# Two expert units multiply three sequence chunks in one float32 pass instead of two, with new engine lists

## The chip, the cores and the metric

The kernel runs on one core of a Trainium2 chip. The metric is the device time of one execution in microseconds (us), the median of several runs. The profile is one more execution, recorded instruction by instruction.

## What is computed

Three stages follow each other: a chunked linear scan (an attention with decay), a gated feed-forward layer, and a second feed-forward layer with a squared ReLU. Cut to what matters:

```python
for c in range(nc):                                   # scan over 768 positions, 4 batches, 8 heads
    M = einsum('bhin,bhjn->bhij', Cc, Bc) * L          # L: decay between positions, causal
    y[:, :, sl] = einsum('bhij,bhjd->bhid', M, xc) + einsum('bhin,bhnd->bhid', Cc, state) * decay_to_i
    state = decay_full * state + sum(Bx)
x = y.transpose(0, 2, 1, 3).reshape(3072, 256)
g = x @ w_gate                                        # 256 x 1536
x = (g * sigmoid(g) * (x @ w_val)) @ w_out            # 1536 x 256
h = maximum(x @ w2_in, 0.0)                           # 256 x 2048
out = (h * h) @ w2_out                                # 2048 x 256
```

The weights arrive as 64-bit words, which the kernel itself turns into float32.

## The kernel before

**The scan.** Each of the four batches is cut into chunks of 112 positions (six, and a last one of 96). A chunk takes, in this order: two transposes of its B and C on TensorE (tile `trb`, L529, from the loaded tile `eb`), the spread of its decays over partitions (`ab`, L616), two scans on VectorE that make `L` (L625), the scores (`cb`, L679), their product with `L` (`mt`, L712), the output product (`ys`, L727), and the transposes of the new state (`turn`, L766), which the next chunk's `ys` needs. So the chunks of a batch follow each other in a chain. The tiles `eb` are two buffers: the load of chunk 2's B and C (L518) goes into the buffer of chunk 0.

**The gated layer of the first batch.** The 1536 hidden columns are six units of gate and value weights (`gv` 0 to 5), each of two blocks of 128. For one block and one piece of positions, TensorE makes the gate product (`g`, L791) and the value product (`v`), ScalarE the SiLU, VectorE the product (L858), and TensorE multiplies it back into the accumulator (`acc`, L905). There are two ways to multiply. Units marked exact use float32 operands as they are (`xf` times `v`, two instructions for the 256 inputs, each of which the trace shows as two records). The others split each operand in a rounded and a rest part (`hi` and `lo`, `xh_all` and `xl_all`) and use three products of parts. Only units 0 and 3 are exact, and only for chunks 0 to 2. The table `cells` says which unit multiplies which chunks: an entry (j, c0, c1, exact) is unit j with chunks c0 to c1 - 1, and the order of the entries is the order of priority. A piece wider than 256 positions takes a PSUM bank each for `g` and `v`, a narrower one takes one for both.

**The other batches** are multiplied in four tiles of 512 positions, and the second layer follows in six tiles of 512; both in split parts.

**Preparing the weights.** Each unit is loaded in two halves (L428) and turned into float32 by ScalarE (L441, L447, and L452 for units so marked) and VectorE (L456, the clamp L462, the shift L466). A string of four digits for each unit in `engs` says: sign on ScalarE, clamp on POOL (GpSimd), rest part on POOL, in halves or whole.

**The order.** A list for each engine (`seq`) names the operations by number, in the order in which the engine issues them. A planner in the kernel gives the buffers. Where the planner has TensorE without work, the program gets dummy products of a tile of zeros (`idle`, L241), a fixed number at each place, written into the tile of the instruction that follows:

```python
for _ in range(fills.pop()):
    nc.tensor.matmul(t, idle[:, : shape[0]], idle[:, : t.shape[-1]], start=True, stop=True)
...
n = (gap - COLD) / 110 + COLD / 216 if free < 1200 else gap / 105
if gap > 150:
    fills.append(int(n) + PLAN["more"] if free < 1200 or op.start > 12000 else int(gap / 216) + 1)
```

They stand in the instruction stream as any other product and run whether TensorE would have waited or not.

Of the kernel before, what the change touches and what calls it, by code (L numbers as in the profile page):

```python
# [141 lines left out]
def kernel(  # L142
# [982 lines left out]
    with tc.manual_schedule():  # L1125
        for op in order:
# [22 lines left out]
        (0, 2, 3, 1),  # L1149
        (3, 1, 3, 1),  # L1150
        (3, 0, 1, 1),
        (2, 0, 3, 0),
        (2, 3, 7, 0),
        (0, 0, 2, 1),
# [9 lines left out]
    engs=['0011', '1001', '1000', '1011', '1011', '1011', '1001', '1000', '0010'],  # L1164
# [7 lines left out]
    rest=[55, 98],  # L1172
# [25 lines left out]
        ],  # L1198
        POOL=[
# [5 lines left out]
        ],  # L1205
        PE=[
# [16 lines left out]
        ],  # L1223
        ACT=[
# [61 lines left out]
```

## Time and profile before

| | |
|---|---|
| median of 3 runs | 627.5 us (627.07 to 627.64) |
| the profiled execution's own time | 627.6 us |
| its span, first to last instruction | 625.9 us |
| TensorE (PE) busy | 619.8 us, 99% of the span |
| VectorE (DVE), ScalarE (ACT), GpSimd (POOL) busy | 424.6, 335.2, 99.4 us |

Busy time is the union of an engine's instructions. The end of a TensorE product is modelled, so its duration is longer than the distance to the next one; what a product costs in a dense stretch is the distance between two starts.

### The profile page before, as it was taken

The page shows a single profiled execution, that of the slowest core. Times are in us where ns is not written, and L with a number is a line of the kernel's source. Part 1 is how long each engine was busy: PE and PEld are TensorE (multiplying, and loading weights), DVE is VectorE, ACT ScalarE, POOL GpSimd, SP SyncE. Part 2 cuts the span into 40 slices and gives each one's busy share as a digit, 9 for nine tenths or more (in the row PEclk, how much of TensorE's full clock was granted, in tenths as well). Part 3 has the DMA queues.
Part 4 walks back from the last instruction along what each step waited for, and adds up shares of the span by engine and source line. Part 5 has one row for each costly group of instructions (what it writes and reads, how often), then busy time and mean ns, then how long its engine had stood idle before and what let it go on. Part 6 is the DMA issues. An engine that isn't in the chain of part 4 may idle for free.

```text
span 625.9 us, 9674 instructions
## 1 busy us (share of the span) xinstructions
PE 619.8 (99%) x3682; PEld 525.1 (84%) x3682; DVE 424.6 (68%) x668; ACT 335.2 (54%) x615; POOL 99.4 (16%) x130
## 2 busy tenths in 40 slices
PE   8999999999999999999999999999999999999997
PEld 6889999998878787878888888888888888888897
DVE  7897888877876866883688985454545554545543
ACT  6898985455443535542476564444444444444443
POOL 2425513313121231211113310000000000000000
PEclk9999999999999999999999999999999999999999
DMA  8879975756656555640224200010010100200101
GB/s 185 212 191 228 209 151 93 132 110 124 135 96 132 99 102 118 148 137 33 68 68 135 68 1 0 1 34 1 9 26 1 35 2 0 35 0 1 34 1 36
DMA packets 153855, 49.85 MB, mean 80 GB/s; under 512 B 141648, under 2 KB 142160, under 8 KB 153808
## 3 DMA queue, kind: packets, MB, share of 16 engines
q1 hardware_dynamic: 153248, 48.87, 35.4%
q8 instruction: 29, 0.48, 0.3%
q10 hardware_dynamic: 560, 0.36, 0.2%
q14 instruction: 18, 0.15, 0.1%
HBM read 34.96 MB, written 3.25 MB: 61 GB/s over the span
## 4 chain that ended last, share of the span: by engine, by line
PE 98%; DMA 1%; DVE 0%; SPq 0%; issue 0%; DVEq 0%
PE h L791 21%; PE g L791 18%; PE acc L977 17%; PE acc L905 16%; PE v L791 14%; PE acc L986 4%; PE ys L727 3%; PE cb L688 2%; PE cb L679 1%; PE ab L616 1%; DMA dv<-in_a_dram 1%; PE trb L529 0%; PE g L241 0%; PE cb L241 0%; PE turn L766 0%; PE ab L241 0%
## 5 line engine op out<-in xcount | busy, mean ns | idle before, releaser
L967 DVE TENSOR_TENSOR p<-t,p 128x512 fp32r<-128x512 f32 x96 | 68.2, 713 | 65.2 <-ACT p L963 65.2
L963 ACT ACTIVATE p<-t 128x512 fp32r<-128x512 f32 x96 | 60.6, 633 | 75.9 <-PE acc L977 53.3
L960 DVE TENSOR_TENSOR t<-t 128x512 f32<-128x512 f32 x96 | 66.2, 691 | 51.6 <-ACT t L957 51.6
L977 PE MATMUL acc<-p,hi 128*128 128x512 f32 x320 | 98.6, 389 | 0.0
L957 ACT ACTIVATE t<-h 128x512 f32<-128x512 f32 x96 | 57.4, 598 | 66.1 <-PE h L791 63.2
L905 PE MATMUL acc<-p,hi 128*128 128x512 f32 (+3 forms) x320 | 90.2, 366 | 0.0
L855 ACT ACTIVATE t<-g 128x512 f32<-128x512 f32 (+5 forms) x88 | 44.8, 516 | 71.9 <-PE g L791 63.9
L791 PE MATMUL h<-xh_all,hi 128*128 128x512 f32 x192 | 74.8, 390 | 0.0
L791 PE MATMUL h<-xl_all,hi 128*128 128x512 f32 x192 | 74.8, 390 | 0.0
L791 PE MATMUL h<-xh_all,lo 128*128 128x512 f32 x192 | 74.7, 389 | 0.0
L878 DVE TENSOR_TENSOR p<-t,p 128x512 fp32r<-128x512 f32 (+3 forms) x80 | 57.4, 727 | 21.0 <-ACT p L873 20.4
L873 ACT ACTIVATE p<-t 128x512 fp32r<-128x512 f32 (+3 forms) x80 | 45.4, 572 | 47.2 <-DVE t L858 38.6
L977 PEld LDWEIGHTS acc<-p,hi 128*128 128x128 f32 x320 | 60.1, 188 | 12.5
L858 DVE TENSOR_TENSOR t<-t,v 128x512 f32<-128x512 f32 (+2 forms) x68 | 43.7, 647 | 36.0 <-PE v L791 26.8
L791 PE MATMUL g<-xh_all,hi 128*128 128x512 f32 (+3 forms) x184 | 65.3, 355 | 0.0
L791 PE MATMUL g<-xl_all,hi 128*128 128x512 f32 (+3 forms) x184 | 64.6, 351 | 0.0
L791 PE MATMUL g<-xh_all,lo 128*128 128x512 f32 (+3 forms) x184 | 64.6, 351 | 0.0
L905 PEld LDWEIGHTS acc<-p,hi 128*128 128x128 f32 x320 | 57.1, 189 | 7.3
L977 PE MATMUL acc<-p,lo 128*128 128x512 f32 x160 | 62.2, 389 | 0.0
L905 PE MATMUL acc<-p,lo 128*128 128x512 f32 (+3 forms) x160 | 57.9, 362 | 0.0
L791 PE MATMUL v<-xh_all,hi 128*128 128x512 f32 (+2 forms) x136 | 51.2, 377 | 0.0
L791 PE MATMUL v<-xl_all,hi 128*128 128x512 f32 (+2 forms) x136 | 51.0, 375 | 0.0
(108 smaller groups left out, 1071.7 us busy)
## 6 DMA issues: line engine op xcount, KB each, us to landing
ab<-decay SPq DMA_DIRECT2D x23, 452.0 KB, 4.2
raw<-in_moe_w_out_dram SPq DMA_DIRECT2D x14, 512.0 KB, 5.5
raw<-in_moe_w_in_dram SPq DMA_DIRECT2D x8, 512.0 KB, 3.8
raw<-in_moe_w_val_dram SPq DMA_DIRECT2D x6, 512.0 KB, 5.2
raw<-in_moe_w_gate_dram SPq DMA_DIRECT2D x6, 512.0 KB, 5.4
xa<-in_x_dram SPq DMA_DIRECT2D x24, 112.0 KB, 3.0
out_dram<-o SPq DMA_DIRECT2D x40, 64.0 KB, 1.9
bc<-in_B_dram SPq DMA_DIRECT2D x18, 56.0 KB, 2.9
```

The source lines that it names most:

```text
L791: nc.tensor.matmul(ps, l, r, start=(i == 0), stop=(i == len(terms) - 1))
L855: nc.scalar.activation(t[:, :n], gg(), AF.Silu)
L858: nc.vector.tensor_tensor(tb.t[:, :n], tb.t[:, :n], vv(), op=ALU.mult)
L873: nc.scalar.activation(p[:, 0, :n], tb.t[:, :n], AF.Copy)
L878: e.tensor_tensor(p[:, 1, :n], tb.t[:, :n], p[:, 0, :n].bitcast(F32), op=ALU.subtract)
L905: nc.tensor.matmul(ps, l, r, start=bank not in done_f, stop=f == NF - 1, skip_group_check=True,)
L957: nc.scalar.activation(new(tb, [P, TN], F32, "t"), ph.t, AF.Relu)
L960: nc.vector.tensor_tensor(tb.t, tb.t, tb.t, op=ALU.mult)
L963: nc.scalar.activation(new(pb, [P, 2, TN], F32R, "p")[:, 0, :], tb.t, AF.Copy)
L967: e.tensor_tensor(pb.t[:, 1, :], tb.t, pb.t[:, 0, :].bitcast(F32), op=ALU.subtract)
L977: nc.tensor.matmul(acc[-1 - i][m], l.t[:, w], pb.t[:, r, :], start=(f == 0 and s == 0), stop=(f == NF2 - 1 and s == 2),)
L986: nc.tensor.matmul(acc[-1 - i][q][:, :256], pb.t[:, l, tk], r, start=(f == 0 and s == 0), stop=(f == NF2 - 1 and s == 2),)
```

## The change

The exact units get one piece of 336 positions (chunks 0 to 2) each, where each had a piece of 112 and one of 224. Unit 0's clamp goes from VectorE to POOL, and the second unit of output weights (`o` 1) is prepared whole and no longer in halves. `rest` changes a bound on the cells that use VectorE for the rest part; with 14 or 12 cells neither 55 nor 99 is reached. All five lists are new.

```diff
     cells=[
         (1, 3, 7, 0),
         (3, 3, 7, 0),
         (4, 3, 7, 0),
-        (0, 2, 3, 1),
-        (3, 1, 3, 1),
-        (3, 0, 1, 1),
+        (3, 0, 3, 1),
         (2, 0, 3, 0),
         (2, 3, 7, 0),
-        (0, 0, 2, 1),
+        (0, 0, 3, 1),
         (5, 3, 7, 0),
...
-    engs=['0011', '1001', '1000', '1011', '1011', '1011', '1001', '1000', '0010'],
+    engs=['0111', '1001', '1000', '1011', '1010', '1011', '1001', '1000', '0010'],
...
-    rest=[55, 98],
+    rest=[99, 98],
...
         DVE=[
-            10, 0, 9, 15, 40, 41, 36, 151, 35, 37, 152, 20, 155, 156, 101, 42, 174, 175, 102, 178,
+            10, 0, 9, 15, 40, 35, 146, 37, 147, 20, 150, 151, 96, 42, 169, 97, 101, 170, 102, 174,
```

On TensorE, after the spread and the scores of the first chunk, the program stands as follows (one piece of the difference, dummies cut to one of each place).

```order
 L529 MATMUL trb<-eye,eb_102 128x128 x2
-L241 LDWEIGHTS idle
-L241 MATMUL ab<-idle 128x256
...
 L616 MATMUL ab<-dv,pick 128x113 x8
+L241 LDWEIGHTS idle
+L241 MATMUL ys<-idle 128x256
```

The three dummies ahead of the second chunk's spread are gone, and five more stand behind it, ahead of the first output product. Over the whole program the dummies are:

| written into | ab | trb | cb | ys | turn | g | sum |
|---|---|---|---|---|---|---|---|
| before | 25 | 5 | 8 | 7 | 6 | 13 | 64 |
| after the change | 19 | 20 | 8 | 24 | 11 | 10 | 92 |

All 28 more stand behind the second chunk's transposes and ahead of the first split product of the gated layer. There the changed program also has the third chunk's transposes right behind the second chunk's scores, ahead of `turn`; before they followed `turn`.

Where the exact products run, among the fourth to seventh chunk's steps, TensorE had (each name `g` is a gate and value product in one bank):

```order
L791 MATMUL g<-xf,v 128x224 x6
L679 MATMUL cb<-bct 128x112 x8
L791 MATMUL g<-xf,v 128x224 x2
L727 MATMUL ys<-mt_96,xa_92 32x128 x8
L529 MATMUL trb<-eye,eb_102 128x128 x2
L791 MATMUL g<-xf,v 128x112 x2
```

and has now:

```order
L529 MATMUL trb<-eye,eb_101 128x128 x2
L679 MATMUL cb<-bct 128x112 x8
L791 MATMUL g<-xf,v 128x336 x2
L791 MATMUL v<-xf,v 128x336 x2
L727 MATMUL ys<-mt_96,xa_92 32x128 x8
L529 MATMUL trb<-eye,eb_102 128x128 x2
```

Counted over the program, 24 products of 112 columns and 24 of 224 have become 24 of 336.

On the queue of loads and stores (SP), the tenth to sixteenth issues; `eb_101` is the buffer that gets chunk 2's B and C here, `xa` the chunks' inputs x, `decay` a store of the prepared decays of one batch. One piece of the difference:

```order
 L507 DMA xa_92<-in_x_dram 112x8x32
+L370 DMA decay<-dv 8x7x113
+L518 DMA eb_101<-in_B_dram 112x8x16
+L518 DMA eb_101<-in_C_dram 112x8x16
 L507 DMA xa_93<-in_x_dram 112x8x32
-L518 DMA eb_101<-in_C_dram 112x8x16
-L518 DMA eb_101<-in_B_dram 112x8x16
-L428 DMA raw<-in_moe_w_out_dram 128x2x512
-L370 DMA decay<-dv 8x7x113
```

The store of the decays, which waits for the second clip of the decays on VectorE (L284), now stands ahead of the loads for chunk 2.

## Rows read from the trace of the kernel before

**Rows 1.** The page: busy time by engine, and the chain that ended last.

```profile
PE 619.8 (99%) x3682; PEld 525.1 (84%) x3682; DVE 424.6 (68%) x668; ACT 335.2 (54%) x615; POOL 99.4 (16%) x130
...
PE 98%; DMA 1%; DVE 0%; SPq 0%; issue 0%; DVEq 0%
```

**Rows 2.** Stretches: busy us (instructions) of PE, PEld, DVE, ACT, POOL; clock; DMA.

```profile
6.00:60.00 54.00, 53.81 (x531) 46.97 (x532) 46.15 (x75) 46.57 (x111) 16.20 (x22) 1.00 0.90 198
60.00:200.00 140.00, 140.00 (x1020) 125.36 (x1019) 113.67 (x206) 82.63 (x166) 40.56 (x55) 1.00 0.66 133
200.00:400.00 200.00, 200.00 (x1049) 162.80 (x1048) 144.58 (x205) 104.44 (x174) 38.58 (x35) 1.00 0.32 80
400.00:622.00 222.00, 222.00 (x1069) 187.46 (x1068) 117.02 (x172) 98.93 (x162) 0.00 (x0) 1.00 0.07 13
```

**Rows 3.** Timeline of TensorE, the start: start us, length us, instruction, count.

```profile
6.19 2.05 PE L616 MATMUL ab<-dv,pick 32*128 32x113 f32 x16 [1.68 <-DVE dv L279]
...
12.37 0.49 PE L241 MATMUL ab<-idle 128*128 128x256 bf16 x3
12.79 1.15 PE L616 MATMUL ab<-dv,pick 32*128 32x113 f32 x16
13.87 0.94 PE L241 MATMUL ys<-idle 128*128 128x256 bf16 x7
14.74 0.64 PE L727 MATMUL ys<-mt,xa 128*32 128x128 f32 x16
15.31 1.15 PE L679 MATMUL cb<-bct 64*128 64x112 f32 x16
```

**Rows 4.** The dummies' tile: count, duration ns min/median/max, first and last start.

```profile
L241 PEld LDWEIGHTS <-idle x64: 95/98/151, 1.1 to 26.4; 128*128 128x128 bf16 x64
```

**Rows 5.** Timeline of TensorE, where the exact and the first split products run.

```profile
35.21 1.68 PE L791 MATMUL g<-xf,v 128*128 128x224 f32 x8
36.73 0.38 PE L529 MATMUL trb<-eye,eb 128*128 128x128 f32 x2
...
40.18 0.61 PE L905 MATMUL acc<-t,v 128*128 128x112 f32 x4
40.62 0.38 PE L766 MATMUL turn<-eye,st 128*16 128x128 f32 x2
...
47.00 0.52 PE L791 MATMUL g<-xh_all,hi 128*128 128x432 f32 x1
...
58.49 0.35 PE L791 MATMUL v<-xh_all,lo 128*128 128x432 f32 x1
58.68 0.32 PE L791 MATMUL v<-xh_all,hi 128*128 128x336 f32 x1
58.84 0.32 PE L791 MATMUL v<-xl_all,hi 128*128 128x336 f32 x1
```

**Rows 6.** Groups by form, 0 to 60 us: shape, count, busy us, mean ns.

```profile
L791 PE MATMUL g<-xf,v 128*128 128x224 f32 x32 | 7.1, 360 | 0.0
L791 PE MATMUL g<-xf,v 128*128 128x112 f32 x32 | 4.4, 276 | 0.0
L905 PE MATMUL acc<-t,v 128*128 128x224 f32 x16 | 3.8, 360 | 0.0
L905 PE MATMUL acc<-t,v 128*128 128x112 f32 x16 | 2.5, 278 | 0.0
```

**Rows 7.** Timeline of SP's issues, and the loads of `eb` from issue to landing.

```profile
10.42 2.14 SPq L518 DMA_DIRECT2D eb<-in_C_dram  x1
12.66 0.85 SPq L518 DMA_DIRECT2D eb<-in_B_dram  x1
...
DMA to landing us min/median/max: 2.1/4.0/5.5
```

**Rows 8.** Timelines of VectorE and POOL: the second clip, a clamp, a rest part.

```profile
11.64 0.70 DVE L284 TENSOR_SCALAR dv<-dv 96x560 f32<-96x560 f32 x2
13.33 0.41 DVE L462 TENSOR_SCALAR v<-v 128x512 f32<-128x512 f32 x1
...
26.61 2.63 POOL L476 TENSOR_TENSOR lo<-v,hi 128x1024 fp32r<-128x1024 f32 x1
```

133 rows, old and new, of tables (ACT, DVE, PE, POOL) are left out of this document.

## The prediction

> **What bounds the kernel now.** I read the shares of the page first. TensorE is busy 99% of the span, and 98% of the chain that ended last is TensorE [rows 1]. A busy TensorE may still wait inside modelled ends, so I went on to the stretches and to the timeline. In the four stretches from 6 us to 622 us its busy time equals the stretch, but for 0.19 us in the first [rows 2]. VectorE and ScalarE have air even in the fullest of them (46 of 54 us). The last idle gap of weight in the timeline is the one of 1.68 us that ends at 6.19 us, when the first decays have come [rows 3]. From there on the distances between starts are those of products that follow each other: a chunk's spread takes 1.08 us (12.79 to 13.87), its output product 0.57, and I saw no distance that a wait would explain. So from 6.19 us to the end the time is the sum of what the TensorE list holds. Dummies are part of that list: 64 of them, each with a weight load of its own [rows 4]. Another engine can only add time here; work taken from VectorE gives nothing back, because TensorE doesn't wait for it.
>
> Two things follow. Every product or dummy added behind 6.19 us is paid in full, and every one removed is gained in full. And a wait added anywhere is paid too, since the dummies do not shrink when TensorE is late.
>
> **The change part by part.**
>
> *Dummies.* The list has 92 instead of 64, and all 28 more stand behind 12.37 us. Their price: three take 0.42 us (12.37 to 12.79) and seven take 0.87 us (13.87 to 14.74) [rows 3], so four more take 0.45 us, 0.11 us each. 28 x 0.11 = +3.08 us.
>
> *Exact products.* Before, 48 records of 112 columns and 48 of 224 (32 and 16 of each) [rows 6]; after, 48 of 336. Four of 112 take 0.44 us (40.18 to 40.62) and eight of 224 take 1.52 us (35.21 to 36.73) [rows 5], which is 0.11 and 0.19 us each, 14.40 us in all. No row has 336 columns in float32. If the price grows with the columns from 224, it is 0.285 us, 13.68 us in all, a gain of 0.72. If it grows by the step from 112 to 224, it is 0.27, 12.96 in all, a gain of 1.44. The split products in the same stretch go from 0.16 us at 336 columns to 0.19 at 432 [rows 5], about as the columns do; and 0.11 at 112 is no dearer than a dummy, so it looks like a floor rather than a point on the line. I take -0.72 us.
>
> The Trainium skill would make that gain smaller. TensorE: Matmul & The Clock Gate, section Back-to-back issue gap, puts the warm distance at N/2.4 + 2.5 ns for each product, and FP8 and Floating Point Precision, section TensorE Precision Notes, has float32 as four passes. By an estimate from both, 336 columns take 0.570 us and 112 and 224 together 0.580, which over 24 is a gain of 0.24 us, and the sum below would be 0.5 us higher. The trace's floor at 112 columns (two records of 0.11 us, against 0.197 by that estimate) does not agree with it.
>
> *Entries into narrow tiles.* The three dummies ahead of a spread took 0.42 us, 0.09 more than their 0.33: the last product ahead of a spread, scores or output product waits a little. The new list has 15 such entries from full tiles in the chunks' part instead of 14: +0.09 us.
>
> *The start.* The lists ahead of the first spread differ on POOL only in order, and the first spread waited for the decays' load; the first twelve issues of SP are the same. I put nothing.
>
> *Loads for chunk 2.* Before, its C and B were issued at 10.42 and 12.66 us [rows 7]. Now the store of the decays is ahead of them, and it waits for the second clip, which ended at 12.34 us (11.64 + 0.70) [rows 8]. Two clamps fewer stand ahead of that clip on VectorE, so I let it end at 11.9. With 0.4 us for the store's issue and the rest for B and C, the later load leaves at about 13.2. From issue to landing these loads take 2.1, 4.0 or 5.5 us (least, median, most) [rows 7], so it lands at 15.3, 17.2 or 18.7. TensorE's list comes to the transposes that need it at 12.37 + 0.09 + 1.08 (spread) + 1.42 (12 dummies and an entry) + 0.57 (output product) + 1.08 (scores, as the spread) + 0.34 (3 dummies) = 16.95 us, with rows 3 for each. The wait is 0, 0.25 or 1.75 us; I take +0.2.
>
> *The clamp on POOL.* No row shows it there. On VectorE it takes 0.41 us; a two-input rest part of twice the size takes 2.63 us on POOL [rows 8]. The second half's clamp starts by about 12.3 us, and VectorE comes to the shift that needs it at about 13.5. With 0.41 it costs nothing; by half of 2.63 (1.3) about 0.1 us of VectorE; with 2.63 about 1.4 us. Queued behind the shift are the second chunk's scans and products, and behind those the second output product. That is reached at 20.85 us by the same kind of sum as above, and its input is ready near 18.7, so 2 us hide it. Price 0; without that cover up to 1.4 us.
>
> *The rest.* `o` 1 prepared whole merges instructions of ScalarE and VectorE and is first read near 39 us, some 3 us after VectorE is through with it: nothing. Merged SiLUs and products save VectorE and ScalarE some instructions, which gives nothing here. `rest` reaches no cell. The first split product started at 47.00 us [rows 5]; the same sum of distances puts it at 49.6 now, with as much exact work done, and the last chunk's rounded and rest parts are ready by about 49.0.
>
> **The sum.** 3.08 - 0.72 + 0.09 + 0.2 = +2.65 us on the profiled execution's own 627.6 us, which is 0.1 above the median of 627.5: **630.2 us**.
>
> **The rivals.**
>
> *A longer wait.* The loads for chunk 2 come at their slowest (1.75 us instead of 0.2), or another input of the chunk chain is late by as much. For it: the new lists were laid out with less room around the chain, and the queue of SP now stands still until the clip. Against it: elsewhere I find 0.6 us or more between an input and its use. It gives 631.7, and with a second such wait 633.
>
> *Width is cheap.* At 0.27 us a record the gain is 1.44, and without the load's wait the time is 629.3.
>
> *Faster.* The place is the 336-column record. The other terms are +3.2 us without the wait; they are paid back when 48 records take 11.2 us, so at 0.233 us each. Within 0.2% of before it would be from 0.26 down, and faster beyond that from 0.207 us. At 0.20, hardly more than 224 columns cost, the time is 626.0. Against it: split products show no such saving from width. For it: only that the row is missing.
>
> *The change does less than it says*: the dummies fall into waits that the trace hides in modelled ends, so that they cost nothing, and only the 0.72 us shows: 627.0. Against it: the distances, not the ends, were added up.
>
> **How the numbers follow.** Forecast (no wait or a small one) 0.68, longer wait 0.15, cheap width at 0.27 0.10, faster 0.03, dummies at no cost 0.04. A run of this kernel tells 0.2%, 1.26 us, from no change. The first three lie beyond it, 0.93 slower. Same gets 0.04 (the hidden waits and the near side of cheap width), faster 0.03. The range goes from 628.9 (cheap width, with some tenths for the terms read to 0.01 us) to 632.5 (between one long wait and two); it leaves out about 0.07 below and 0.07 above.
>
> **What would show it.** Right: 92 dummies at 0.11 us; float32 rows of 336 columns at 0.28 to 0.29 us; the first split product near 49.6; TensorE busy over the whole of 6 to 622 us; a distance of some tenths, if any, ahead of the third transposes near 17 us. Wrong: gaps on TensorE between 17 and 60 us with VectorE, ScalarE or a load as the releaser; 336 columns far from 0.285; or the first split product at 47 as before.

## The result, and the profile after

The changed kernel takes 632.6 us (median of 5 runs, 630.98 to 633.78), the kernel before took 627.6 beside it (627.07 to 628.62). The ratio is 1.0066, with a 95% interval of 1.0053 to 1.0079: slower by about 4.1 us (the two medians lie 4.9 us apart). The profiled execution is the shortest of the five, 630.98 us with a span of 629.3 us, which is 3.4 us above the profiled one of before.

The page (busy time by engine, and the chain that ended last), against [rows 1]:

```profile
PE 622.4 (99%) x3662; PEld 521.4 (83%) x3662; DVE 426.6 (68%) x660; ACT 335.5 (53%) x608; POOL 104.0 (17%) x132
...
PE 96%; DMA 1%; DVE 1%; SPq 1%; ACT 0%; issue 0%; DVEq 0%
```

TensorE is busy 2.6 us more, with 20 records fewer, and 2% more of the chain is now with other engines. The dummies, against [rows 4], and the exact products by form in the first 60 us, against [rows 6]:

```profile
L241 PEld LDWEIGHTS <-idle x92: 95/98/153, 1.1 to 49.5; 128*128 128x128 bf16 x92
```

```profile
L791 PE MATMUL v<-xf,v 128*128 128x336 f32 x16 | 5.4, 459 | 0.0
L791 PE MATMUL g<-xf,v 128*128 128x336 f32 x16 | 5.3, 453 | 0.0
L905 PE MATMUL acc<-t,v 128*128 128x336 f32 x16 | 5.2, 459 | 0.0
```

There are 92 dummies and 48 exact records of 336 columns, as the lists have them. The stretches, against [rows 2]:

```profile
6.00:60.00 54.00, 53.33 (x496) 40.62 (x494) 44.16 (x63) 44.75 (x100) 20.52 (x22) 0.97 0.87 190
60.00:200.00 140.00, 139.83 (x1022) 125.26 (x1021) 115.04 (x206) 83.20 (x168) 39.28 (x54) 1.00 0.66 135
```

Still dense (and full from 200 to 622 us, as before), but there is a first gap behind 60 us (139.83 of 140.00; it was 140.00). Ahead of 60 us the 0.67 us that are missing are nearly all one wait, for a load ahead of the first transposes (0.62 us at 7.80 below). The timeline of TensorE, against [rows 3] and [rows 5]:

```profile
5.60 1.15 PE L616 MATMUL ab<-dv,pick 32*128 32x113 f32 x16 [1.12 <-DVE dv L279]
...
7.80 0.66 PE L529 MATMUL trb<-eye,eb 128*128 128x128 f32 x2 [0.62 <-DMA eb<-in_B_dram]
...
10.09 1.64 PE L679 MATMUL cb<-bct 64*128 64x112 f32 x16
...
12.32 1.15 PE L616 MATMUL ab<-dv,pick 32*128 32x113 f32 x16
...
16.81 0.55 PE L529 MATMUL trb<-eye,eb 128*128 128x128 f32 x2
17.19 1.36 PE L241 MATMUL turn<-idle 128*128 128x256 bf16 x11
...
40.86 1.30 PE L791 MATMUL g<-xf,v 128*128 128x336 f32 x4
42.00 1.29 PE L791 MATMUL v<-xf,v 128*128 128x336 f32 x4
...
49.59 0.44 PE L791 MATMUL g<-xh_all,hi 128*128 128x432 f32 x1
```

The first split product stands at 49.59 us, where 49.6 was predicted. Four exact records of 336 columns take 1.14 us (40.86 to 42.00), 0.285 each, as taken. The third transposes take 0.38 us to the next start (16.81 to 17.19), where two of them without a wait take 0.21 or 0.22: a wait of 0.17, where 0.2 was put. The loads behind it, on SP, against [rows 7]:

```profile
12.52 0.32 SPq L370 DMA_DIRECT2D decay<-dv  x1
12.96 0.32 SPq L518 DMA_DIRECT2D eb<-in_B_dram  x1
13.32 0.56 SPq L518 DMA_DIRECT2D eb<-in_C_dram  x1
```

The later one leaves at 13.32 us; 13.2 was predicted. The second clip on VectorE with the shift (L466) ahead of it, and the first of the two clamps, now on POOL, against [rows 8]:

```profile
10.17 0.69 DVE L466 SCALAR_TENSOR_TENSOR v<-v,raw 128x512 uint32<-128x512 uint32 x1 [0.88 <-POOL v L462]
...
11.79 0.70 DVE L284 TENSOR_SCALAR dv<-dv 96x560 f32<-96x560 f32 x2
...
8.22 1.92 POOL L462 TENSOR_SCALAR v<-v 128x512 f32<-128x512 f32 x1 [2.48 <-ACT v L441]
```

The clip ends at 12.49 us, later than the 11.9 put for it: the shift ahead of it waits 0.88 us for the first clamp on POOL.

What the prediction did not have stands at 65 us. TensorE at the scores (`cb`, L688) and the product behind them, first of the kernel before, then of the changed one:

```profile
61.96 0.57 PE L688 MATMUL cb<-bct 128*128 128x112 bf16 x8
62.34 0.44 PE L791 MATMUL v<-xh_all,hi 128*128 128x432 f32 x1
```

```profile
64.39 0.57 PE L688 MATMUL cb<-bct 128*128 128x112 bf16 x8
65.12 0.47 PE L791 MATMUL v<-xh_all,hi 128*128 128x432 f32 x1 [0.17 <-DVE t L858]
```

POOL, VectorE and ScalarE ahead of that, in the changed kernel:

```profile
60.98 2.42 POOL L476 TENSOR_TENSOR lo<-v,hi 128x1024 fp32r<-128x1024 f32 x1
```

```profile
61.54 2.32 DVE L878 TENSOR_TENSOR p<-t,p 128x432 fp32r<-128x432 f32 x1
64.46 1.12 DVE L858 TENSOR_TENSOR t<-t,v 128x432 f32<-128x432 f32 x2 [0.60 <-ACT t L855]
...
63.90 0.53 ACT L855 ACTIVATE t<-g 128x432 f32<-128x432 f32 x1 [1.85 <-DVE p L878]
```

From the end back: TensorE waits for VectorE's `t`, VectorE for ScalarE's SiLU, ScalarE 1.85 us for VectorE's rest part L878, and that took 2.32 us beside a rest part on POOL that ended at 63.40. The marked wait is 0.17 us; from start to start the eight scores take 0.73 us, where they took 0.38 before. The kernel before has such a pair at the same place, a rest part on POOL from 60.29 to 62.69 us and beside it

```profile
61.29 1.77 DVE L878 TENSOR_TENSOR p<-t,p 128x336 fp32r<-128x336 f32 x1 [0.46 <-ACT p L873]
```

but there TensorE did not wait behind it. So the pair is not new; what is new is that the product TensorE needs next hangs behind it.

The end differs too. The last product (timeline), then what SP waited for and what the queue of instruction loads (q14) moved from there to the end: packets, MB, share of 16 engines. First before, then after:

```profile
622.34 0.28 PE L986 MATMUL acc<-hi,p 128*128 128x256 f32 x1
...
SPq L1281 <- DMA out_dram<-o: 1.0, 3, 0.4
...
q14 instruction: 1, 0.01, 0.9%
```

```profile
625.19 0.28 PE L986 MATMUL acc<-hi,p 128*128 128x256 f32 x1
...
SPq L1278 <- DMA out_dram<-o: 1.5, 3, 1.1
...
q14 instruction: 2, 0.02, 1.7%
```

From the last product to the end of the span (625.9 and 629.3 us) it is 3.56 us before and 4.11 after. The longest wait of SP for the last stores to land is 1.1 us instead of 0.4, and two packets of instructions are loaded there instead of one. So of the 3.4 us, 2.85 lie ahead of the last product and 0.55 behind it.

### The profile page after: what moved, and what is told of

The parts are those of the page before. It is cut to its first block, busy times and chain, and to the rows that moved or that the text cites. A ratio compares the mean times of both kernels' runs of the same rounds, so it can differ in the third digit from the quotient of the medians.

```text
span 629.3 us, 9620 instructions
## 1 busy us (share of the span) xinstructions
PE 622.4 (99%) x3662; PEld 521.4 (83%) x3662; DVE 426.6 (68%) x660; ACT 335.5 (53%) x608; POOL 104.0 (17%) x132
## 4 chain that ended last, share of the span: by engine, by line
PE 96%; DMA 1%; DVE 1%; SPq 1%; ACT 0%; issue 0%; DVEq 0%
PE h L791 21%; PE acc L977 17%; PE g L791 17%; PE acc L905 16%; PE v L791 14%; PE acc L986 4%; PE ys L727 2%; PE cb L688 2%; PE cb L679 1%; PE ab L616 1%; DMA eb<-in_C_dram 0%; DMA dv<-in_a_dram 0%; PE ys L241 0%; DVE p L878 0%; PE trb L241 0%; SPq L428 0%
## 5 line engine op out<-in xcount | busy, mean ns | idle before, releaser
L855 ACT ACTIVATE t<-g 128x512 f32<-128x512 f32 (+3 forms) x84 | 44.7, 535 | 74.3 <-PE g L791 64.0
L878 DVE TENSOR_TENSOR p<-t,p 128x512 fp32r<-128x512 f32 (+3 forms) x80 | 60.0, 761 | 21.4 <-ACT p L873 20.9
L858 DVE TENSOR_TENSOR t<-t,v 128x512 f32<-128x512 f32 (+2 forms) x72 | 45.5, 638 | 34.9 <-PE v L791 24.3
```

The lines of the kernel that those rows point to most:

```text
L855: nc.scalar.activation(t[:, :n], gg(), AF.Silu)
L858: nc.vector.tensor_tensor(tb.t[:, :n], tb.t[:, :n], vv(), op=ALU.mult)
L878: e.tensor_tensor(p[:, 1, :n], tb.t[:, :n], p[:, 0, :n].bitcast(F32), op=ALU.subtract)
```

## The experiments

All times are medians, beside runs of the kernel before on the same chip (its median there 628.2 to 628.4). In the experiments on the number of dummies and on the order of a list, the formula for dummies is replaced by a table of counts by operation, so that nothing else moves.

**The changed kernel again** (no edit).

> The changed kernel once more, to see whether what stands above the sum of its TensorE list is in every execution. Prediction's theory (a dense list, +2.65 us): 2.6 us above the kernel before in this call, and in the trace the first split product at 49.6 us with no wait ahead of it. Rival (a longer wait in some executions, which the first profile, the shortest of five runs, does not show): 4 to 5 us above, and in a trace whose span is near 631 us one wait of about 1.5 us on TensorE that the first trace lacks, at the third transposes near 17 us or among the first 12 us.

632.19 us against 628.38, ratio 1.0061 (1.0048 to 1.0073): +3.8 us. Behind the first spread the trace has the same waits as the first one and none of 1.5 us; the first spread starts at 5.99 instead of 5.60 us. What differs most between executions is the start. Sorted by the mean granted clock of the run:

| mean clock | before, 17 runs | changed kernel, 6 runs |
|---|---|---|
| 0.997 to 0.999 | 627.50 to 628.18 (8 runs) | 631.24 (1) |
| 1.0 | 628.38 to 629.10 (6) | 631.79 to 632.42 (4) |
| below 0.996 | 628.90 to 629.17 (3) | 633.63 (1) |

Both kernels have the spread. Within the first two rows the difference is about 3.5 us, in the third 4.6. The first comparison had more of the short kind for the kernel before (627.07 to 627.64 thrice of five) than for the changed one. Whether the new lists meet the longer kinds more often is open: of all 34 runs with these lists and 92 dummies, 6 lie at 0.996 to 0.999, of the 57 runs of the kernel before beside them 28; with 64 dummies it is 7 of 12, and no run shows why. What a mean of 1.0 can look like, the trace of a later run shows (the one with the loads first, below):

```profile
5.90 2.05 PE L616 MATMUL ab<-dv,pick 32*128 32x113 f32 x16 [1.40 <-DVE dv L279]
...
10.77 2.06 PE L679 MATMUL cb<-bct 64*128 64x112 f32 x16
...
13.30 1.15 PE L616 MATMUL ab<-dv,pick 32*128 32x113 f32 x16
...
17.79 0.38 PE L529 MATMUL trb<-eye,eb 128*128 128x128 f32 x2
18.00 1.36 PE L241 MATMUL turn<-idle 128*128 128x256 bf16 x11
```

The first spread and the first scores take 2.05 and 2.06 us there, against 1.15 and 1.64 in the first trace, and the second spread starts at 13.30 instead of 12.32 us: about 1 us, most of it from the level of the clock in the first 13 us. (The mean of 1.0 is no contradiction: the clock column shows 1.00 for the whole of that start, although the 16 products of a spread take 2.05 us there as they do at the lower level elsewhere; so it does not count the start.) Not every run at 1.0 is of this kind: the trace with the exact products split (below) has the second spread at 12.40 us and loses 0.6 us to a load later. A wait of 1.5 us, as the rival has it, stands in none of these traces.

**The kernel before with 28 dummies more.**

```diff
+if not exact and not extra:
+    extra.append(1)
+    for _ in range(28):
+        nc.tensor.matmul(pg.t[:, :256], idle[:, :P], idle[:, :256], start=True, stop=True)
```

> The kernel before with 28 dummies of the same size in one row ahead of its first split product, near 47 us. Prediction's theory (every dummy behind 6.19 us is paid): 28 x 0.11 = +3.1 us, first split product near 50.1 us. Rival (dummies fall into waits that the modelled ends hide): 0 to +0.5 us.

631.29 us, ratio 1.0045 (1.0033 to 1.0057): +2.8 us. The trace:

```profile
47.53 3.22 PE L826 MATMUL g<-idle 128*128 128x256 bf16 x28
50.50 0.44 PE L791 MATMUL g<-xh_all,hi 128*128 128x432 f32 x1
```

2.97 us for 28, 0.106 each. The dummies alone, in the old program, cost nearly all of what was predicted for them.

**The changed kernel with 64 dummies.** The counts, by the tile they are written into:

```diff
-ab 19, trb 20, cb 8, ys 24, turn 11, g 10
+ab 17, trb 11, cb 8, ys 14, turn 6, g 8
```

> The changed kernel with 64 dummies instead of 92, all 28 taken from the places behind 12.37 us in about equal parts. Prediction's theory (a dense list): -3.1 us against the changed kernel, so between 0.5 us below and 1.5 us above the kernel before. Rival (the dummies cover waits of the chunk chain that are there anyway): 0 to -1 us against the changed kernel, and in the trace waits in the dummies' place, on VectorE or on loads.

629.29 us, ratio 1.0019 (1.0010 to 1.0027): 2.9 us below the changed kernel, 0.9 to 1.2 above the kernel before. So with as many dummies as before and cheaper exact products it is still slower, and the rest of the change costs about 1.2 + 0.6 = 1.8 us (0.6 is the measured gain of the products, next run). Its trace names parts of that (who waits for whom: us in all, times, longest):

```profile
PE trb L529 <- DMA eb<-in_B_dram: 1.0, 2, 0.7
PE ys L727 <- ACT hi L472: 0.3, 1, 0.3
```

Of the 1.0 us, 0.34 are at the third transposes near 17 us; there and at `ys` the dummies had covered a part. From start to start the third transposes lose 0.66 us in this trace (0.99 from 16.17 to 17.16, where one dummy and two transposes take 0.33), the scores near 62 us 0.36, and the end 0.53: with 0.3 at `ys`, about the 1.8 us.

**Exact products split again.**

```diff
-product(ps, terms)
+for c0, c1 in [(0, 224), (224, n)] if exact else [(0, n)]:
+    product(ps[:, c0:c1], [(l, r[:, c0:c1]) for l, r in terms])
```

(and the same for the products into `acc`)

> The changed kernel with each exact product of 336 columns made as one of 224 and one of 112, as the kernel before had them; order, dummies and loads as in the changed kernel. Prediction's price (336 columns 0.285 us, 224 and 112 together 0.30): +0.7 us against the changed kernel. Rival of cheap width (0.27 us): +1.4 us. If the products lie beside other waits: 0.

632.12 us, ratio 1.0065 (1.0052 to 1.0078): no difference from the changed kernel that its spread would show. The trace resolves it:

```profile
41.66 1.35 PE L791 MATMUL g<-xf,v 128*128 128x224 f32 x8
42.85 1.37 PE L791 MATMUL v<-xf,v 128*128 128x224 f32 x8
```

Eight records (four of 224 and four of 112, shown as one group) take 1.19 us where four of 336 took 1.14: 0.05 for each of 12 such groups, 0.6 us in all. The price of 0.285 us holds; cheap width (1.4 us) is refuted.

**Loads for chunk 2 first** (their two operations ahead of the store in SP's list).

```diff
-142, 21, 182, 184, 166, 80, 82,
+142, 184, 182, 166, 80, 21, 82,
```

> The changed kernel, its 92 dummies held, with the loads for chunk 2 on SP ahead of the store of the decays again; the store stands behind the first load of w_out. Prediction's price of that step: -0.2 us against the changed kernel, and no wait at the third transposes near 17 us. Rival of the longer wait (the executions that were not traced lose 1 us or more there): -1 us or more against the changed kernel.

632.48 us, ratio 1.0073 (1.0055 to 1.0090): no gain that shows beside the start's spread. In its trace, above, the third transposes take 0.21 us (17.79 to 18.00) and no longer 0.38. That alone doesn't price the step, because its second spread comes late, at 13.30 us. In the trace with the rest part later (below), the store is ahead of the loads and the second spread comes at 13.06, and there is no wait either:

```profile
17.55 0.38 PE L529 MATMUL trb<-eye,eb 128*128 128x128 f32 x2
17.76 1.36 PE L241 MATMUL turn<-idle 128*128 128x256 bf16 x11
```

Where the store is ahead and the second spread comes at 12.32 to 12.67 us, the third transposes lose 0.17 us (the first trace), 0.13 (the second) and 0.59 (the products split, where 0.29 are marked):

```profile
17.34 0.51 PE L529 MATMUL trb<-eye,eb 128*128 128x128 f32 x2 [0.29 <-DMA eb<-in_B_dram]
17.69 1.36 PE L241 MATMUL turn<-idle 128*128 128x256 bf16 x11
```

So the step costs 0 to 0.6 us, by when TensorE comes and how long the load takes. A longer wait of 1 us or more stands in no trace with 92 dummies.

**The clamp on VectorE again.**

```diff
-engs=['0111',
+engs=['0011',
```

(and its two operations moved from POOL's list to VectorE's)

> The changed kernel, its 92 dummies held, with the clamp of unit 0 on VectorE again, as in the kernel before. Prediction's price of the move: 0, so no difference from the changed kernel. Rival (the clamp on POOL, 1.9 us each in the trace after, makes VectorE late and so TensorE): -0.5 us or more.

631.87 us, ratio 1.0055 (1.0043 to 1.0067): no difference that shows. On POOL the clamps took 1.92 and 1.96 us, and VectorE waited 0.88 and 0.50 us for them; TensorE lost about 0.1 us by it, at the second spread (0.43 us behind the transposes ahead of it, where 0.31 is the least in these traces). On VectorE they push the second clip back further, and the second spread waits for that:

```profile
PE ab L616 <- DVE dv L284: 0.7, 1, 0.7
```

**The rest part on POOL later.**

```diff
-290, 502, 298, 485, 504, 489,
+290, 502, 485, 504, 298, 489,
```

> The changed kernel, its 92 dummies held, with one rest part on POOL (the one at 60.98 us in the trace after, 2.42 us) moved behind the two products of the second batch's preparation that follow it. Theory: beside it VectorE's rest product (L878, 61.54 us) takes 2.32 instead of 0.6 us, ScalarE's SiLU waits for that, and TensorE for the SiLU's product; with the rest part later, L878 takes about 0.6 us there and the wait of 0.17 us at 65.1 us is gone, with -0.2 to -0.4 us on the distance from the products at 62 us to the last one. Rival: the wait has another cause and stays, or the late rest part makes TensorE wait for it: no gain or a loss.

631.73 us, ratio 1.0062 (1.0048 to 1.0076). The trace shows what was asked:

```profile
62.11 0.60 DVE L878 TENSOR_TENSOR p<-t,p 128x432 fp32r<-128x432 f32 x1
63.31 1.12 DVE L858 TENSOR_TENSOR t<-t,v 128x432 f32<-128x432 f32 x2 [0.60 <-ACT t L855]
...
64.96 0.57 PE L688 MATMUL cb<-bct 128*128 128x112 bf16 x8
65.34 0.44 PE L791 MATMUL v<-xh_all,hi 128*128 128x432 f32 x1
```

L878 takes 0.60 us instead of 2.32, and the scores to the next product 0.38 instead of 0.73: 0.35 us of TensorE's list was POOL and VectorE side by side. The gain did not reach the end of this trace: from the first split product to the last it is 575.21 us instead of 575.60, but from there to the end 4.42 instead of 4.11, so together 579.63, as in the two traces of the changed kernel (579.71 and 579.60). The ratios, 1.0062 and 1.0061, do not show it either; the runs at a mean clock of 1.0 alone (631.00 to 631.87 us, against 631.79 to 632.42) leave room for it. Whether the longer end belongs to the edit, one trace does not tell. The Trainium skill has this: SBUF — State Buffer, section Who interferes with whom, says that a VectorE instruction with two inputs in SBUF contends with a GpSimd instruction that reads SBUF, that the shared port pair is an exclusive lock, and that the order of issue decides who blocks. The trace agrees: POOL's rest part started first (60.98 against 61.54), and L878 ended at 63.86 us, 0.46 behind the end of the rest part, as if nearly all of it ran after that.

**Without the dummies behind 12.37 us**, in the changed kernel and in the kernel before (28 left in each).

> The changed kernel with 28 dummies, those ahead of 12.37 us; the 64 behind are left out, 36 more than in the run with 64. If the list were dense without them too: 64 x 0.11 = -7.0 us against the changed kernel, so 3 us faster than before. If the dummies stand where the chunk chain waits anyway: little beyond what 28 fewer gave (-2.8 us), and in the trace waits on VectorE, ScalarE or loads where they stood. My guess lies between: -4.5 us, and the granted clock may fall where TensorE waits.

> The kernel before with 28 dummies, those ahead of 12.37 us; the 36 behind are left out. Paid in full: 36 x 0.11 = -4.0 us against the kernel before. If they cover waits of the chain: 0 to -2 us, with waits in the trace where they stood. My guess is -2 us; if it is below -1.3 us it beats both kernels.

The changed kernel: 631.57 us (628.61 to 635.56), ratio 1.0049 (1.0032 to 1.0067): 2.3 us slower than with 64 by the medians, 1.9 by the ratios. All of that is in nine of the 12 runs, at a mean clock of 0.980 to 0.992; the three at 0.997 took 628.61 to 629.88 us, as with 64. The kernel before: 626.91 us, ratio 0.9987 (0.9968 to 1.0005), by the ratio a gain of 0.8 us that its interval does not settle, with one run at 632.85. In the stretches of the changed one (the columns as in [rows 2]; the run traced is one at 0.992):

```profile
18.00:24.00 6.00, 4.90 (x54) 3.63 (x52) 4.64 (x7) 3.97 (x11) 2.46 (x8) 0.59 0.84 193
24.00:30.00 6.00, 6.00 (x44) 4.06 (x45) 4.61 (x9) 4.45 (x13) 2.22 (x5) 0.56 1.03 200
```

TensorE waits 1.1 us for a load and 1.1 for VectorE's `mt` where dummies stood; behind that the granted clock is at its lower level (1.2 GHz) for most of 18 to 30 us, so that scores take 2.05 us that take 1.15 at the upper one. With 64 dummies the clock column shows 1.00 in both stretches. My guess of -4.5 us was wrong: dummies behind which a wait lies also hold the clock.

**A version meant to beat both**: the kernel before with 41 dummies.

```diff
-ab 25, trb 5, cb 8, ys 7, turn 6, g 13
+ab 15, trb 5, cb 8, ys 7, turn 6
```

> A version meant to beat both: the kernel before with 41 dummies. The 3 ahead of the second spread, the 7 ahead of a later spread and the 13 ahead of the first exact products are left out; the 7 ahead of the first output product and the 6 ahead of the first state transposes stay, since in the run with 28 a load made the first output product wait 1.0 us. 23 x 0.11 = -2.5 us if paid in full; with the waits of 0.3 to 0.5 us that the run with 28 showed later, -1.6 to -2.0 us against the kernel before. If the missing dummies only become waits: 0 to -1 us.

626.14 us, ratio 0.9977 (0.9965 to 0.9988): 2.0 us faster by the medians, 1.4 by the ratio. It beats both kernels. Two of its 12 runs, at a mean clock of 0.991, took 628.4 and 628.5 us. The trace is of one of them; its clock column shows 0.50 from 8 to 18 us, and the second spread takes 2.05 us as well.

## Why the prediction was right, and where its sum was short

The sign and the mechanism were right: TensorE's list is the time, and the list became longer. The sum was short, +2.65 us against +3.4 in the profiled pair, +3.8 in the larger comparison and +4.1 in the first.

- **Dummies, +3.08.** Right: 28 in a row cost 2.97 us, alone +2.8 in the time.
- **Exact products, -0.72.** Right in price (0.285 us a record); undone it is 0.6 us in the trace. The rivals cheap width and faster fall with it. The gain of 0.24 us, estimated in the prediction from the Trainium skill (TensorE: Matmul & The Clock Gate, section Back-to-back issue gap), is less than half of what was measured. The section gives that formula for a product by itself and says that it counts too little for narrow ones; here two records of 336 columns come out as estimated (0.570 us), two of 112 take 0.22 us instead of 0.197.
- **Loads for chunk 2, +0.2.** Right in size: 0.17 us in the first trace, 0 to 0.6 in the five with this order and 92 dummies; issue at 13.32 where 13.2 was taken. The clip was 0.6 us later than put, since the shift ahead of it waited for the clamp on POOL, and the issue only 0.1. The rival of a longer wait (1.75 us) came in none of these traces.
- **The clamp on POOL, 0.** Right within what the times show (0.1 us in the trace), though its duration was nearer to the far bound (1.92 and 1.96 us of at most 2.63), and the prediction looked only at what stands behind the second shift, not at the clip behind the first.
- **Entries, +0.09**, were not measured by themselves.
- **The start, 0.** A spread of about 1 us in both kernels, most of it from the clock's level. That the kernels do not differ in it is not shown: the first spread starts at 5.60 to 6.29 us in the eight traces with the changed lists and at 6.05 to 6.35 in the four with the old ones, and the kinds of run are mixed otherwise (6 of 34 and 28 of 57, above). The median of five runs carries the spread: the forecast was right about the shorter kind of run (630.98 against 630.2); the median was of the other kind, and lies 0.1 above the range.
- **The rest, 0: this step failed.** It said that merged work on VectorE gives nothing and costs nothing. In the new lists a product that TensorE needs soon hangs behind L878, which a rest part on POOL slows, and TensorE waits 0.35 us more at 65 us. The lists for it were there: the prediction looked for waits up to 60 us.
- **The end, not in the sum.** 0.4 to 0.8 us from the last product to the end in all eight traces with the changed lists (3.95 to 4.42 us) that the four with the old ones lack (3.54 to 3.60), whatever the dummies. The traces show where: SP waits for the last stores to land, 0.8 to 1.2 us at the longest in the eight and 0.4 in the four. In the same stretch the eight load two packets of instructions on q14 and the four load one. That the second packet holds the stores up is likely by this, but no run moved it, and why it falls there with the new lists stays open.

With the rest and the end added, 2.97 - 0.6 + 0.17 + 0.35 + 0.55 = 3.44 us, beside a profiled difference of 3.4. That it fits so well is in part luck: two more differences of this pair are not in it, the second chunk's transposes, which start 0.26 us earlier than before (11.89 and 12.15), and the 0.1 us at the second spread. With both it is 3.3.

## What to carry to other kernels

Where TensorE is dense, price a change by its list, record by record, and do not expect filler to shrink by itself: 0.106 us a dummy was paid in full. Filler has two uses that must be told apart by removing it: some hides nothing (in the kernel before, 23 of 64 could go for 1.4 to 2 us), some stands where a wait is and holds the clock (in the changed kernel, 36 fewer than 64 cost about 2 us). And when lists are laid out anew, look at which two-input VectorE instructions come to stand beside GpSimd ones and who waits behind them, far behind the edit too. Follow a gain to the end of the span: in the one trace of it, the 0.35 us won at 65 us did not arrive there.

## What the hardware showed that was not expected

- Executions differ by up to about 1 us through the level of TensorE's clock in the first 13 us (first spread 1.15 or 2.05 us, first scores 1.15 to 2.06), and the mean granted clock of the run can be *higher* in the longer kind (1.0 against 0.997), since the start is not counted in it.
- Behind waits of 1.1 us each that ended near 17.6 and 20.4 us the granted clock went to its lower level for most of 18 to 30 us, although TensorE was busy 6.00 of 6 us in the second half of that.
- A rest part on VectorE (L878) of 0.60 us took 2.32 us beside one GpSimd instruction.
- The last stores landed late in the eight traces in which a second packet of instructions was loaded behind the last product (SP's longest wait 0.8 to 1.2 us, 0.4 in the four others).
